# Tile 24's normalizer steps made one tile later in a one-core attention decode kernel

## The chip, the cores and the metric

The kernel runs on one core of a Trainium2 chip. The metric is the device time of one execution in microseconds (us), as the median of several runs. Beside it stands one execution taken by the hardware profiler, with every instruction of the five engines: TensorE (PE; PEld is its weight load), VectorE (DVE), ScalarE (ACT), GpSimd (POOL) and SyncE (SP, which here only issues DMAs). Times inside the profile count from the start of its span.

## The reference

One transformer layer for one new token in each of four batch rows: a condition vector gives shifts, scales and gates; attention over a cache of 4096 keys and values for 32 heads of 128; then a small gated MLP. Nearly all work and nearly all bytes are in the attention:

```python
q = (h @ wq).reshape(B, 1, 32, 128).transpose(0, 2, 1, 3)
scores = einsum('bhqd,bhkd->bhqk', q, k_cache) * 128 ** -0.5
p = softmax(scores, axis=-1)
o = einsum('bhqk,bhkd->bhqd', p, v_cache)
x = x + ga * (o.reshape(B, 1, 4096) @ wo)
x = x + gb * mlp(layernorm(x) * (1 + cb) + sb)
```

Everything is bf16. The two caches are 4 x 32 x 4096 x 128 values each, 268 MB together; the whole kernel reads 282.73 MB from HBM.

## The kernel before

The attention is cut into `NT` = 32 tiles. A tile is 4.19 MB of keys and as much of values, laid out as 128 partitions x 128 keys x 128 (`NJ` = 128 keys in each partition). The first `N0` = 24 tiles come in pairs: tiles 2k and 2k+1 together are 8 heads of one batch row, their scores are made one tile after the other and their softmax and value product once for the pair (after the odd tile). Tiles 24 to 31 are single: 4 heads each, with a softmax and a value product of their own. Tile 24 is the first of these.

The order of the work on every engine is the order in which the program's lines issue it (a manual schedule): one loop over the tiles from line 701. Each engine takes its own list in order, and an instruction that waits holds up those behind it on that engine alone. In iteration i the steps that matter here are:

- `mult(i, 0)`, `mult(i, 1)` (L393, VectorE): keys times query, half a tile (64 keys) each, 128 x 8192 elements.
- `reduce_d` (L401, TensorE): sums products over part of the head dimension into a PSUM tile `red`; `sum8` (L424, VectorE) finishes the sum into the score tile `S`; `sum_rest` (L413, VectorE) sums the last 48 keys of the tile without TensorE.
- `scores(i - 1)` (L437 to L454, VectorE): row maximum and what the exponential needs; it then calls `exps`.
- `exps` (L467, ScalarE): the exponentials, written as bf16 into the weight tile `pbd`, with their row sums into `rs`. Pairs use the whole of `pbd`; single tiles use a quarter of it each, and need the rest to be zero.
- `pv` (L519, TensorE): the value product. `PV_START`, `PV_MID` and `PV_END` say in which iteration it stands.
- `norm_r` (single tiles: L487, VectorE, `rsb` = `maskd` times `rs`; pairs: L481, POOL), `norm_a` (L497, TensorE, sums `rsb` over partitions into `z`) and `norm_b` (L504, VectorE, the reciprocal `rz`). `o_scale` (L566 for single tiles) multiplies the value product by `rz`. These three steps are what the change moves.

Before the change `norm_r(i - 1)` and `norm_a(i - 1)` stand in iteration i, and `norm_b(i - 2)` near its start. Iteration 25 is special, because the layout of `pbd` changes there from pairs to single tiles: the value product of the last pair (`PV_MID`, tile 23) must have read `pbd`, then POOL sets it to zero (L732), and only then the exponentials of tile 24 are issued; `scores(24)` has left them out:

```python
if i in PV_MID:
    pv(PV_MID[i])
if i == N0 + 1:
    load_v(N0)
    load_v(N0 + 1)
    nc.gpsimd.memset(pbd8, 0.0)
    nc.vector.memset(opss[0], 0.0)
    exps(N0)
```

All bulk loads are issued by SP on one queue, in the order of the `load_...` calls; each waits on SP until its buffer is free. Keys go into buffers `bufA` and `bufB` in turn (8.39 MB each), values into `bufC`; the values of tiles 30 and 31 go into `bufB` behind the keys of tiles 30 and 31, and the weights of the end (`wo`, `win`, `wout`, `wg`) into `bufA`. The last loads in the queue are, in order: the values of tile 30 (4.19 MB), those of tile 31 in five pieces (32, 32, 32, 16 and 16 keys: 1.05 MB three times, 0.52 MB twice), `win` in two (0.92 MB each, L602), `wout` (0.92 MB, L603) and `wg` in two (0.39 and 0.13 MB, L605).

After the loop comes the tail: the last scores, value products and the projection with `wo` (`o_last` L555, `o_proj` L613), the second layer norm, the MLP's first product with `win` (L884), its second with `wout` (L909), the gate `gb` from `wg` (L917), some ten small VectorE steps to L954, and the output's DMA (L955).

Of the kernel before, what the change touches and what calls it, by code (L numbers as in the profile page):

```python
# [54 lines left out]
def kernel(  # L55
# [32 lines left out]
    N0 = 2 * B * GP  # L88
# [25 lines left out]
    def ps_sm(shape, dtype=F32):  # L114
        return psum.tile(shape, dtype, name="sm", bufs=3)
# [42 lines left out]
    def load_v(i):  # L158
        if i < N0:
            load(bufC, kv_view(A_v_cache, i), (NP,))  # L160
        else:
            load(vts[i], kv_view(A_v_cache, i), TAIL if i == L else (NJ,))
# [220 lines left out]
    def pair(i):  # L383
        return i < N0

    def ends(i):
        return i >= N0 or i % 2 == 1

    def mult(i, kc):
        kt = kts[i][:, kc * KC:(kc + 1) * KC, :]  # L390
        g, b = divmod(i // 2 if pair(i) else i - N0, B)
        q = (qbp if pair(i) else qbo)[:, g, b, :]
        nc.vector.tensor_tensor(out=kt, in0=kt, in1=bc(q, KC), op=ALU.mult)  # L393

    def reduce_d(i, kc):
        ns = on_pe(i, kc)
        rd = 512 // ns
        kt = kts[i][:, kc * KC:kc * KC + ns, :]
        red = ps_red().rearrange("p (n r) -> p n r", r=rd)
        for m in range(DH // rd):  # L400
            nc.tensor.matmul(  # L401
                red, lhsT=ident_bf, rhs=kt[:, :, m * rd:(m + 1) * rd],
                start=(m == 0), stop=(m == DH // rd - 1),
            )
        st[i, "red", kc] = red
# [23 lines left out]
    def scores(i):  # L429
        sum8(i, 1)  # L430
        S = st.pop((i, "S"))
        if not ends(i):
            return
        if pair(i):
            S = st["both"]
        mrow = wk.tile([P, 1], F32, name="mrow")
        nc.vector.tensor_reduce(out=mrow, in_=S, axis=AX.X, op=ALU.max)  # L437
        mb = wk.tile([P, R], F32, name="mb", bufs=1)
        if pair(i):
            nc.vector.scalar_tensor_tensor(  # L440
                out=mb, in0=mrow.to_broadcast([P, R]), scalar=-att_scale,
                in1=fars.rearrange("p h u -> p (h u)"), op0=ALU.mult, op1=ALU.add,
            )
        else:
            nc.vector.tensor_scalar(
                out=mb, in0=mrow.to_broadcast([P, R]), scalar1=-att_scale, scalar2=None, op0=ALU.mult
            )
        mt = wk.tile([P, R], F32, name="mt", bufs=1)
        nc.vector.transpose(mt, mb)
        nM = wk.tile([P, 1], F32, name="nM")  # L450
        nc.vector.tensor_reduce(out=nM, in_=mt, axis=AX.X, op=ALU.min)  # L451
        if pair(i):
            nb = wk.tile([P, 2], F32, name="nb")
            nc.vector.tensor_scalar(out=nb, in0=far, scalar1=nM, scalar2=None, op0=ALU.add)  # L454
            nM = nb
        st[i, "in"] = S, nM
        if i != N0:
            exps(i)
# [14 lines left out]
    def norm_r(i):  # L473
        if not ends(i):
            return
        rs = st.pop((i, "rs"))
        if pair(i):
            g, b = divmod(i // 2, B)
            if b == 0:
                st["P", g, "rsb"] = wk.tile([P, B, HQ, 2], F32, name="rsb8")  # L480
            nc.gpsimd.tensor_tensor(  # L481
                out=st["P", g, "rsb"][:, b], in0=maskd[:, :, None].to_broadcast([P, HQ, 2]),
                in1=rs[:, None, :].to_broadcast([P, HQ, 2]), op=ALU.mult,
            )
            return
        st[i, "rsb"] = wk.tile([P, HQ], F32, name="rsb")
        nc.vector.tensor_scalar(out=st[i, "rsb"], in0=maskd, scalar1=rs, scalar2=None, op0=ALU.mult)  # L487

    def norm_a(i):
        if not pair(i):  # L490
            rsb = st.pop((i, "rsb"))
        elif i % (2 * B) == 2 * B - 1:
            rsb = st.pop(("P", i // 2 // B, "rsb")).rearrange("p b q h -> p (b q h)")
        else:
            return
        z = ps_sm(list(rsb.shape))
        nc.tensor.matmul(z, lhsT=inv_d, rhs=rsb, start=True, stop=True)  # L497
        st[i, "z"] = z

    def norm_b(i):  # L500
        if (i, "z") in st:
            z = st.pop((i, "z"))
            rz = wk.tile(list(z.shape), F32, name=f"rz{z.shape[1]}", bufs=2 if pair(i) else 4)
            nc.vector.reciprocal(out=rz, in_=z)  # L504
            st[i, "rz"] = rz
# [4 lines left out]
    def pv(i):  # L510
        n = (NP if pair(i) else NJ) // G
        pv_some(i, 0, n, n)
# [11 lines left out]
    def o_pick(i):  # L524
        ops = ops_of(i)
        sel = sels[HP if pair(i) else HQ]
        osb = wk.tile([P, DH], F32, name="osb", bufs=2)
        nc.vector.tensor_scalar(  # L528
            out=osb, in0=ops[:, 0, :], scalar1=sel[:, 0:1], scalar2=None, op0=ALU.mult
        )  # L530
        for g in range(1, G):
            nc.vector.scalar_tensor_tensor(  # L532
                out=osb, in0=ops[:, g, :], scalar=sel[:, g:g + 1], in1=osb,
                op0=ALU.mult, op1=ALU.add,
            )
        st[i, "osb"] = osb
# [109 lines left out]
    def dealt(k):  # L646
        pp = st.pop(("pp", k))
        n = pp.shape[1]
        ow = own if n == HP else own[:, 0:n * B, 0:n]
        nc.vector.tensor_tensor(  # L650
            out=ow, in0=pp.rearrange("p r b h -> p (r b) h"),
            in1=bc(mask8 if n == HP else mask4, n * B), op=ALU.mult,
        )
        od = late.tile([P, n, B], BF16, name=f"od{k}")
        with nc.allow_low_precision("all but one term of each sum are zero"):
            nc.vector.tensor_reduce(
                out=od.rearrange("p r b -> p (r b)"), in_=ow, axis=AX.X, op=ALU.add
            )
        st["od", k] = od
# [31 lines left out]
    def o_add(wp, b0, b1):  # L691
        a = acc[:, :, b0:b1]
        nc.vector.tensor_tensor(out=a, in0=a, in1=wp, op=ALU.add)
# [3 lines left out]
    def add_up():  # L697
        while adds:
            o_add(*adds.pop(0))

    for i in range(NT):
        mult(i, 0)
        if i >= 1:
            scores(i - 1)
        if i >= 2:
            norm_b(i - 2)
        todo = PICKS.get(i, (i - 3,) if i % 2 == 0 and 4 <= i <= N0 + 2 else ())
        t = PV_START.get(i, i - 2 if i % 2 and 3 <= i < N0 else None)
        if t is not None:
            pv(t)  # L710
        if i % 2 and i < N0:
            load_v(i)
        if i == L:
            dealt(1)
            dealt(2)
        reduce_d(i, 0)
        for t in todo:
            o_pick(t)
            o_cols(t)
        if i == 0:  # L720
            late_mod_b()
        if i == N0 + 2:
            nc.vector.memset(opss[1], 0.0)
        if i == L:
            project()
            deal(GP)
# [8 lines that stand above are left out]
        if i == L - 1:  # L735
            deal(0)
        mult(i, 1)
        if i >= 1:
            norm_r(i - 1)
        for t in todo:  # L740
            o_scale(t)
        sum8(i, 0)
        if i == L - 1:
            dealt(0)
        if i == L:
            rows_out()
            dealt(GP)
            o_pick(L - 3)
        reduce_d(i, 1)
        sum_rest(i)  # L750
        if i >= 1:
            norm_a(i - 1)
        if i == L - 1:
            deal(1)
            deal(2)
        if i == L:
            o_cols(L - 3)
            turn()
        if i in PV_END:
            if i == N0 + 3:  # L760
                load_v(N0 + 2)
            pv(PV_END[i])
        if i == L:
            o_scale(L - 3)
        if i % 2 and i + 3 < N0:
            load_k(i + 3)
        elif i == N0 - 3 or i == N0 - 1 or i == N0 + 1:
            load_k(i + 3)
            load_k(i + 4)
        elif i == N0 + 3:  # L770
            load_v(N0 + 3)
            load_k(L - 1)
            load_k(L)
        elif i == L - 2:
            load_wo()
            late_consts()
            load_v(L - 3)
            load_v(L - 2)
        elif i == L - 1:
            load_v(L - 1)  # L780
        elif i == L:
            load_v(L)
            load_end()
# [202 lines left out]
```

## Time and profile before

| | |
|---|---|
| median of 3 runs | 668.81 us (668.15 to 669.12) |
| the profiled execution | 668.59 us, its span 666.8 us |
| VectorE busy | 577.0 us (87% of the span), 437 instructions |
| TensorE busy | 315.9 us (47%), weight loads 137.1 us (21%) |
| ScalarE, GpSimd busy | 154.9 us (23%), 18.5 us (3%) |
| the bulk-load queue | 282.73 MB, its packets 98.4% of 16 engines' span |
| mean granted TensorE clock | 0.75 of full speed |

The profiled execution lies 1.79 us above its span; that remainder is outside what the profile sees. Busy shares are means over the whole span, so they do not say which engine a stage waits for; that is read from the idle time ahead of an instruction, which the trace prints in square brackets with what ended it ("[6.63 <-ACT pbd L467]": idle for 6.63 us until ScalarE's L467 was done).

### The profile page before, as it was taken

How to read it: one execution, taken by the hardware profiler on the slowest of the kernel's cores; microseconds unless marked ns; L12 is line 12 of the kernel's file. 1: busy time of each engine (PE TensorE's matmuls, PEld its weight loads, DVE VectorE, ACT ScalarE, POOL GpSimd, SP SyncE). 2: the span in 40 equal slices, each digit the busy share in tenths (PEclk: the TensorE clock that was granted, in tenths of full speed). 3: DMA queues.
4: the chain of work that ended last, by engine and by line, in shares of the span. 5: the costliest groups of instructions: out<-in, count | busy, mean ns of one | idle time of the engine just before them, and what ended most of it. 6: DMA issues, size and time to landing. Idle time of an engine off the chain costs nothing.

```text
span 666.8 us, 5276 instructions
## 1 busy us (share of the span) xinstructions
PE 315.9 (47%) x2136; PEld 137.1 (21%) x2136; DVE 577.0 (87%) x437; ACT 154.9 (23%) x287; POOL 18.5 (3%) x55
## 2 busy tenths in 40 slices
PE   1565363645253464524245452524536144544996
PEld 0222121212021121211112120211212012221445
DVE  3249999999898998989799897989997799999934
ACT  1210605032050604114060410506060111111112
POOL 3000000000000000000000000000000000004000
PEclk9988787867568786756778675777876688776986
DMA  8999999999999999999999999999999999999994
GB/s 362 452 441 413 440 437 437 433 441 441 436 436 429 418 436 440 433 429 434 436 440 433 436 426 429 441 440 410 440 440 420 436 426 429 439 419 433 437 413 167
DMA packets 10222, 283.09 MB, mean 425 GB/s; under 512 B 972, under 2 KB 2900, under 8 KB 4052
## 3 DMA queue, kind: packets, MB, share of 16 engines
q1 hardware_dynamic: 10176, 282.73, 98.4%
q8 instruction: 17, 0.28, 0.1%
q14 instruction: 9, 0.07, 0.0%
q10 hardware_dynamic: 20, 0.01, 0.0%
HBM read 282.73 MB, written 0.00 MB: 424 GB/s over the span
## 4 chain that ended last, share of the span: by engine, by line
DMA 46%; DVE 35%; PE 15%; ACT 3%; issue 1%; POOL 0%; SPq 0%; DVEq 0%; ACTq 0%
DMA bC<-in_A_v_cache_dram 29%; DMA bB<-in_A_k_cache_dram 12%; DVE S L413 12%; DVE bB L393 10%; PE ops L519 8%; DVE bA L393 6%; PE red L401 3%; DMA bC<-in_w_mod_dram 3%; DVE S L424 2%; ACT pbd L467 2%; DVE osb L532 2%; DMA bC<-in_B_b_sp_dram 1%; PE sm L668 1%; PE qps L326 1%; PE sm L318 1%
## 5 line engine op out<-in xcount | busy, mean ns | idle before, releaser
L467 ACT ACTIVATE pbd<-S,nb 32x256 bf16<-32x256 f32 x96 | 123.5, 1520 | 338.4 <-DVE nb L454 311.1
L401 PE MATMUL red<-bB,ident_bf 128*128 128x512 bf16 x344 | 97.9, 443 | 123.8 <-DVE bB L393 123.8
L401 PE MATMUL red<-bA,ident_bf 128*128 128x512 bf16 x332 | 96.7, 451 | 124.4 <-DVE bA L393 124.4
L401 PEld LDWEIGHTS <-ident_bf 128*128 128x128 bf16 x676 | 74.3, 111 | 364.7 <-issue 232.4
L393 DVE TENSOR_TENSOR bA<-bA,qbp 128x8192 bf16<-128x8192 bf16 x24 | 105.9, 4413 | 19.7 <-DMA bA<-in_A_k_cache_dram 19.7
L393 DVE TENSOR_TENSOR bB<-bB,qbp 128x8192 bf16<-128x8192 bf16 x24 | 106.0, 4418 | 11.2 <-DMA bB<-in_A_k_cache_dram 11.2
L519 PE MATMUL ops<-bC,pbd 128*32 128x512 bf16 (+1 forms) x960 | 79.7, 502 | 54.8 <-DMA bC<-in_A_v_cache_dram 49.7
L413 DVE TENSOR_REDUCE S<-bA 128x48 f32<-128x6144 bf16 x15 | 98.1, 6543 | 0.0
L413 DVE TENSOR_REDUCE S<-bB 128x48 f32<-128x6144 bf16 x14 | 91.6, 6544 | 0.0
L519 PEld LDWEIGHTS <-pbd 128*32 128x32 bf16 (+1 forms) x1008 | 34.1, 119 | 99.8 <-issue 50.0
L467 ACT ACTIVATE pbd<-S,nM 32x128 bf16<-32x128 f32 x32 | 18.5, 578 | 123.6 <-DVE nM L451 80.3
L467 ACT ACTIVATION_READ_ACCUMULATOR pbd<-S,nb 32x1 f32 x96 | 46.9, 489 | 0.0
L424 DVE TENSOR_REDUCE S<-red 128x64 f32<-128x512 f32 x64 | 43.7, 684 | 2.2 <-PE red L401 2.2
L393 DVE TENSOR_TENSOR bA<-bA,qbo 128x8192 bf16<-128x8192 bf16 x8 | 35.3, 4412 | 0.0
L393 DVE TENSOR_TENSOR bB<-bB,qbo 128x8192 bf16<-128x8192 bf16 x8 | 35.3, 4412 | 0.0
L481 POOL TENSOR_TENSOR rsb<-maskd,rs 128x8 f32<-128x8 f32 x12 | 2.4, 200 | 490.7 <-ACT pbd L467 490.7
L532 DVE SCALAR_TENSOR_TENSOR osb<-ops,m,osb 128x128 f32<-128x128 f32 x36 | 12.6, 351 | 1.3
L497 PE MATMUL sm<-rsb,inv_d 128*128 128x4 f32 (+1 forms) x22 | 4.5, 280 | 15.8 <-POOL rsb L481 12.0
L532 DVE SCALAR_TENSOR_TENSOR osb<-ops,selg,osb 128x128 f32<-128x128 f32 x24 | 8.4, 351 | 0.8
L528 DVE TENSOR_SCALAR osb<-ops,selg 128x128 f32<-128x128 f32 x8 | 2.7, 340 | 6.8 <-PE ops L519 6.8
L497 PEld LDWEIGHTS sm<-rsb,inv_d 128*128 128x128 f32 x22 | 4.7, 236 | 18.8 <-POOL rsb L481 13.5
L467 ACT ACTIVATION_READ_ACCUMULATOR pbd<-S,nM 32x1 f32 x32 | 8.1, 252 | 0.0
(164 smaller groups left out, 157.9 us busy)
## 6 DMA issues: line engine op xcount, KB each, us to landing
bA<-in_A_k_cache_dram SPq DMA_DIRECT2D x6, 4096.0 KB, 37.3
bC<-in_A_v_cache_dram SPq DMA_DIRECT2D x6, 4096.0 KB, 28.0
bB<-in_A_k_cache_dram SPq DMA_DIRECT2D x3, 4096.0 KB, 36.9
bC<-in_A_wq_dram SPq DMA_DIRECT2D x1, 4096.0 KB, 12.5
bB<-in_A_k_cache_dram SPq DMA_DIRECT2D x2, 2048.0 KB, 37.0
bB<-in_A_v_cache_dram SPq DMA_DIRECT2D x1, 4096.0 KB, 19.1
bA<-in_A_wo_dram SPq DMA_DIRECT2D x3, 1024.0 KB, 31.2
bB<-in_A_v_cache_dram SPq DMA_DIRECT2D x3, 1024.0 KB, 17.9
```

The lines of the kernel that those rows point to most:

```text
L318: nc.tensor.matmul(qr[R * q:R * (q + 1)], lhsT=hT[:, k, :], rhs=wq_v[:, k, gs, q, :], start=(k == 0), stop=(k == DJ - 1), tile_position=(0 ...
L326: nc.tensor.matmul(qp[:, 0:npair], lhsT=eb2[k][:, b].rearrange("p k q r -> p (k q r)"), rhs=qrow[:, h, k:2 * npair:2], start=(k == 0), sto ...
L393: nc.vector.tensor_tensor(out=kt, in0=kt, in1=bc(q, KC), op=ALU.mult)
L401: nc.tensor.matmul(red, lhsT=ident_bf, rhs=kt[:, :, m * rd:(m + 1) * rd], start=(m == 0), stop=(m == DH // rd - 1),)
L413: nc.vector.tensor_reduce(out=st[i, "S"][:, n0:NJ], in_=kts[i][:, n0:NJ, :], axis=AX.X, op=ALU.add)
L424: nc.vector.tensor_reduce(out=st[i, "S"][:, kc * KC:kc * KC + on_pe(i, kc)], in_=st.pop((i, "red", kc)), axis=AX.X, op=ALU.add,)
L467: nc.scalar.activation(out=pbd8[r, :, 2 * q + h] if pair(i) else pbds[r, i % 4, :, q], in_=S[r, :], func=AF.Exp, bias=nM[r, h:h + 1], scal ...
L497: nc.tensor.matmul(z, lhsT=inv_d, rhs=rsb, start=True, stop=True)
L519: nc.tensor.matmul(ops_of(i)[g:g + rows], lhsT=pb[:, n, :], rhs=vt[:, n, :], start=(m < 4), stop=(m >= end - 4), tile_position=(0, g),)
L528: nc.vector.tensor_scalar(out=osb, in0=ops[:, 0, :], scalar1=sel[:, 0:1], scalar2=None, op0=ALU.mult)
L532: nc.vector.scalar_tensor_tensor(out=osb, in0=ops[:, g, :], scalar=sel[:, g:g + 1], in1=osb, op0=ALU.mult, op1=ALU.add,)
L668: nc.tensor.matmul(wp, lhsT=od[:, r, :], rhs=wo_sb[:, k * HP + r, :], start=(k == 0 and r == 0), stop=(k == GP - 1 and r == HP - 1),)
```

## The change

For tile 24 alone, `norm_r`, `norm_a` and `norm_b` are issued one iteration later, with those of tile 25 and ahead of them. `normed_in(i)` lists the tiles whose product and sum are issued in iteration i: none in iteration 25, tiles 24 and 25 in iteration 26, and i - 1 in every other. The reciprocals follow one iteration behind: tile 24's is made in iteration 27 instead of 26. Nothing is added or removed. Lines below the new function move by five.

```diff
+    def normed_in(i):
+        if i <= 0 or i == N0 + 1:
+            return ()
+        return (i - 2, i - 1) if i == N0 + 2 else (i - 1,)
+
     for i in range(NT):
         mult(i, 0)
         if i >= 1:
             scores(i - 1)
-        if i >= 2:
-            norm_b(i - 2)
+        for k in normed_in(i - 1):
+            norm_b(k)
...
         mult(i, 1)
-        if i >= 1:
-            norm_r(i - 1)
+        for k in normed_in(i):
+            norm_r(k)
         for t in todo:
             o_scale(t)
         sum8(i, 0)
...
         reduce_d(i, 1)
         sum_rest(i)
-        if i >= 1:
-            norm_a(i - 1)
+        for k in normed_in(i):
+            norm_a(k)
```

## The prediction

> **What bounds the kernel now.** I read first the stages around the change, as busy time, granted TensorE clock, DMA share and bytes per stretch (columns: stretch; its length; busy us and instruction count of PE, PEld, DVE, ACT and POOL; clock; DMA share; GB/s):
>
> ```profile
> 447.20:513.40 66.20, 29.83 (x168) 12.17 (x172) 65.39 (x44) 20.62 (x32) 0.40 (x2) 0.70 1.00 430
> 513.40:520.10 6.70, 3.31 (x48) 1.26 (x40) 0.07 (x2) 2.30 (x8) 1.80 (x1) 1.00 1.04 450
> 520.10:600.00 79.90, 35.58 (x223) 15.22 (x224) 78.81 (x64) 9.27 (x32) 0.00 (x0) 0.74 1.00 429
> 600.00:641.00 41.00, 30.52 (x186) 14.89 (x189) 34.96 (x52) 5.98 (x21) 7.05 (x8) 0.82 1.01 429
> 641.00:654.00 13.00, 10.15 (x135) 4.83 (x128) 5.65 (x22) 1.01 (x4) 0.00 (x0) 0.76 1.01 418
> 654.00:658.80 4.80, 3.80 (x64) 3.53 (x65) 1.88 (x11) 0.82 (x4) 1.04 (x5) 0.50 0.70 250
> ```
>
> Two things are full. VectorE is busy 65.39 of 66.20 us before 513.4 and 78.81 of 79.90 after 520.1, and in the 6.70 us between it does nothing. The 16 DMA engines are full throughout (share 1.00 to 1.04 up to 654), in the very gap too. Two chains thus run side by side at almost one pace: the list of VectorE, and the stream of bytes.
>
> The timeline of that gap gives its cause (start, us, engine, line; in brackets the idle time before and what ended it):
>
> ```profile
> 509.03 4.41 DVE L393 TENSOR_TENSOR bA<-bA,qbo 128x8192 bf16<-128x8192 bf16 x1
> ...
> 512.11 3.64 PE L519 MATMUL ops<-bC,pbd 128*32 128x512 bf16 x64
> ...
> 515.82 1.80 POOL L732 MEMSET pbd<- 128x2048 bf16 x1 [15.71 <-PE ops L519]
> ...
> 519.45 0.57 ACT L467 ACTIVATE pbd<-S,nM 32x128 bf16<-32x128 f32 x1
> ...
> 520.06 0.23 DVE L487 TENSOR_SCALAR rsb<-maskd,rs 128x4 f32<-128x4 f32 x1 [6.63 <-ACT pbd L467]
> 520.20 0.68 DVE L424 TENSOR_REDUCE S<-red 128x64 f32<-128x512 f32 x1
> ...
> 520.80 6.54 DVE L413 TENSOR_REDUCE S<-bA 128x48 f32<-128x6144 bf16 x1
> ```
>
> Tile 24's product (L487) is VectorE's next instruction after `mult(25, 1)`, and needs row sums that come only when tile 23's value product has read `pbd` (to 515.8), POOL has cleared it (517.6) and ScalarE has made four exponentials (520.0). Behind it stand L424 and L413, whose inputs were ready: the sum on TensorE ended at 512.17.
>
> Last the end of the stream: the issues of the last loads with their time from issue to landing, and what SP's queue waited for.
>
> ```profile
> bA<-in_B_w_in_dram SPq DMA_DIRECT2D x2, 896.0 KB, 14.3
> ...
> bA<-in_B_w_out_dram SPq DMA_DIRECT2D x1, 896.0 KB, 16.5
> bA<-in_w_mod_dram SPq DMA_DIRECT2D x1, 384.0 KB, 15.1
> ...
> bA<-in_w_mod_dram SPq DMA_DIRECT2D x1, 128.0 KB, 12.9
> ```
>
> SP issued `wout` at 640.99 and `wg` at 643.44 and 645.94 (SP's timeline), so these land at 657.5, 658.5 and 658.8. The same SP rows were held, by the table of SP's waits, until values of tiles 30 and 31 had landed: tile 30 at 640.99, the first two pieces of tile 31 at 643.4 and 645.9.
>
> **The change, step by step.** *Removed:* the stall. VectorE goes from `mult(25, 1)` (ends 513.44) straight to L424 and L413: -6.63 us on its list. L424 carries a wait on ScalarE in the changed program's list, because its score buffer was tile 23's two tiles back; those exponentials ended at 499.8. That this kind of wait is for two tiles back and not for tile 24 shows in the same step one tile earlier: L424 at 495.19 ran without idling while ScalarE was in the middle of tile 23's exponentials (489.4 to 499.8). So 0.
>
> *Moved:* one L487 (0.13 us of list, from 539.66 to 539.79), one pair of PE passes (L497, 0.28 us) and one reciprocal (L504, 0.09 us) go one tile later; each is still done once, so VectorE's sum does not change. In their new place L487 stands behind `mult(26, 1)`, which ends about 533; both tiles' exponentials are done by then (tile 24's at 520.0, tile 25's some 2.4 us after their start near 526.8). The reciprocals stand 11 us behind their PE passes, and `o_scale` of tile 24 wants the result another tile later (578.1 before). No DMA moves and SP's list is unchanged. Cost 0; were the cover gone, the price would be these rows, 0.5 us.
>
> *What is late next.* With VectorE 6.63 us earlier, do the keys still come in time? Counting back from tile 30's values at 641.0, one tile's 4.19 MB at 429 GB/s being 9.78 us: keys 26 land at 513.9 (wanted at 527.26 - 6.63 = 520.6), keys 27 at 523.7 (540.7), keys 28 at 553.0 (558.2), 29 at 562.8 (578.7), 30 at 592.1 (596.2), 31 at 601.9 (611.8). Values 24 and 26 land at 533.4 and 572.5 for value products that would start at 534.2 and 572.9; TensorE's next work for VectorE is 7 us behind the end of each, so a short wait there costs nothing. So VectorE keeps its 6.63 us to the end of tile 31.
>
> There the stream takes over. It is full in every stretch before 654, always with one or two loads waiting in the queue, so earlier issues do not make a byte land sooner, and the last loads keep their landing times. What each allows against its user in the old trace:
>
> - values of tile 30: 641.0, used by L519 at 646.42: 5.4 us
> - second piece of tile 31: 645.94; its matmuls are the last 8 of a group of 48 (646.35 to 650.80), so they begin about 650.1: 4.1 us
> - third piece: not shown; 1.05 MB behind the second at 418 GB/s, 648.4, used at 652.17: 3.7 us, of which 0.6 us is forgiven, since TensorE then idles 0.7 us before L226
> - `wout`: 657.5, used by L909 at 661.56: 4.06 us
> - `wg`: 658.8; its last four matmuls would run about 662.7 and are wanted by VectorE's L950 at 663.59: 3.9 to 4.4 us
>
> So the least is 4.06 us, at `wout`, and the end moves by -4.06 instead of -6.63; the rest turns into waits for DMA in the tail. Small waits that meet (pieces 2 and 3, `wout`) may cost 0.1 us more: I take -4.0. Bounds for this step: -6.63 (no landing in the way), and nothing (below). In the profiled execution's own time 668.59 - 4.0 = 664.6; the median shown is 0.22 higher, so **664.8 us**.
>
> The Trainium skill (DMA: Bandwidth & Descriptors, Specifications) gives the 16 engines a ceiling of 435 GB/s. Stretches here average 418 to 450, so the trace roughly agrees. By that figure the 7.47 MB behind tile 30's values would take 17.2 us instead of the 17.8 seen (641.0 to 658.8), and the sum would be -4.6 at most: the page speaks against the whole 6.63.
>
> **Rivals.** *The stall pays in full*, 668.81 - 6.63 = 662.2. It needs the last loads to land 2.6 us sooner. For it: the last 3 us of the stream run at 0.70 of the engines' share, and some of that might close up. Against it: share 1.00 for 200 us; a fuller queue has nothing to fill. 12 in 100.
>
> *No difference* (within 0.2%, that is 1.34 us, about what a measurement of this kernel can tell from no change), 668.2. Now the end hangs on landings, so a stream 0.4% slower (2.7 of 659 us) eats the 4.0 down to 1.3; or the stall stays whole because L424's wait is for tile 24 after all (668.8, 3 in 100, against the row at 495.19). For it: stretches differ by several per cent. Against: the stream is given the same loads in the same order. 12 in 100.
>
> *Slower*, by one mechanism: TensorE's granted clock between 622.9 and 651. The row of that clock stands at 1.00 from 622 to 638 and at 0.50 after 654. Groups of one kind cost more at the lower clock: a value product of 32 matmuls 1.90 us against 3.34, 16 sums 3.61 against 4.90 to 6.35. In the tail TensorE would now stand idle for landings. If that stage ran at the lower clock throughout: one value product +1.4, two sums of 16 +2.6 to +5.5, the projection's 24 matmuls +2.0 to +4.1, together +6.0 to +11.0. It decides once it exceeds the 6.63 pulled forward, and gives 668.2 to 673.2, say 670.5. Against it: the waits for landings come after 640, behind this stage, and everything ahead moves together. 6 in 100. The Trainium skill (TensorE: Matmul & The Clock Gate, Part 1) says the array runs at half clock until activity releases it, which would be the cause; the trace's 0.50 in idle stretches agrees.
>
> **How the numbers follow.** Forecast 70 in 100 (its own range 663.6 to 666.4: -5.2 to -2.4), full gain 12, no difference 12, slower 6. Faster by over 0.2%: 82; within: 12; slower: 6. The range, 662.2 to 667.2, takes in the full gain and, on the other side, a stream 0.36% slower than before (2.4 us of 659) on top of the forecast.
>
> **What would show it.** Right: no idle time before L424 of tile 25; VectorE's `mult(31, 1)` at about 619.6 instead of 626.2; new waits for DMA on TensorE at the values of tiles 30 and 31 and at `wout`; the last landing still near 658.8 with some 4 us behind it instead of 8. Wrong: a landing of `wg` near 656 (full gain), or the last landing moved later, or VectorE idle before keys 28 or 30.

## The result, and the profile after

The changed kernel takes 664.74 us (median of 6 runs, 664.6 to 666.45) against 668.37 us before (6 runs, 668.15 to 669.12): the ratio is 0.9948, 95% interval 0.9935 to 0.9961. The profiled execution takes 664.6 us with a span of 662.8 us; before it was 668.59 and 666.8. So the span is 4.0 us shorter and the median 3.6 us (by the interval 2.6 to 4.3), where the stall that was taken away was 6.63 us long.

VectorE's timeline in iterations 25 and 26 (start, us, engine, line) no longer shows a gap:

```profile
508.85 4.41 DVE L393 TENSOR_TENSOR bA<-bA,qbo 128x8192 bf16<-128x8192 bf16 x1
513.18 0.68 DVE L424 TENSOR_REDUCE S<-red 128x64 f32<-128x512 f32 x1
513.77 6.54 DVE L413 TENSOR_REDUCE S<-bA 128x48 f32<-128x6144 bf16 x1
...
532.57 0.35 DVE L487 TENSOR_SCALAR rsb<-maskd,rs 128x4 f32<-128x4 f32 x2
```

L424 and L413 follow `mult(25, 1)` at once, without a bracket, and both tiles' products stand together at 532.57, again without a wait. The second half of the last tile's keys (`mult(31, 1)`) is reached at 619.26 instead of 626.20, 6.9 us sooner; 0.2 us of that were there ahead of the change (508.85 against 509.03).

The stages of the changed kernel, in the same stretches as before (length; busy us of PE, PEld, DVE, ACT, POOL; clock; DMA share; GB/s):

```profile
513.40:520.10 6.70, 3.25 (x48) 1.31 (x41) 6.70 (x2) 2.31 (x8) 1.80 (x1) 1.00 1.03 445
520.10:600.00 79.90, 35.82 (x223) 15.37 (x223) 78.81 (x64) 9.27 (x32) 3.88 (x4) 0.76 1.00 429
600.00:641.00 41.00, 34.53 (x218) 16.46 (x218) 30.17 (x59) 6.97 (x24) 3.16 (x5) 0.83 1.01 429
641.00:654.00 13.00, 9.39 (x156) 6.20 (x156) 5.18 (x24) 0.50 (x2) 1.05 (x5) 0.76 1.02 419
654.00:658.80 4.80, 4.07 (x105) 3.67 (x106) 2.03 (x11) 3.77 (x8) 0.00 (x0) 0.50 0.69 242
```

VectorE now works through the first of them (6.70 of 6.70 us). The DMA columns are the old ones within 4%: 429, 429 and 419 GB/s where there were 429, 429 and 418. The stream of bytes landed when it had before: SP issued tile 30's values 6.9 us sooner (at 615.07 instead of 621.92), and they landed at 641.0 both times. What moved is the work around it, and TensorE's timeline in the tail shows where the two meet:

```profile
641.04 3.60 PE L519 MATMUL ops<-bB,pbd 128*16 128x512 bf16 x40 [1.49 <-DMA bB<-in_A_v_cache_dram]
645.90 0.61 PE L519 MATMUL ops<-bB,pbd 128*16 128x512 bf16 x8 [1.25 <-DMA bB<-in_A_v_cache_dram]
...
648.35 0.96 PE L555 MATMUL qps<-pbd,bB 128*128 128x4 bf16 x32 [0.61 <-DMA bB<-in_A_v_cache_dram]
...
650.79 0.59 PE L555 MATMUL qps<-pbd,bB 128*128 128x4 bf16 x16 [0.46 <-DMA bB<-in_A_v_cache_dram]
...
657.48 0.91 PE L914 MATMUL qps<-bC,bA 128*128 128x8 bf16 x28
```

The same places in the kernel before:

```profile
646.35 4.45 PE L519 MATMUL ops<-bB,pbd 128*16 128x512 bf16 x48
...
652.17 0.94 PE L555 MATMUL qps<-pbd,bB 128*128 128x4 bf16 x32
...
655.13 0.57 PE L555 MATMUL qps<-pbd,bB 128*128 128x4 bf16 x16
...
661.56 0.89 PE L909 MATMUL qps<-bC,bA 128*128 128x8 bf16 x28
```

Four groups of products that waited for no DMA before now wait for values of tiles 30 and 31, and the MLP's second product (L914, L909 before) starts at 657.48. Its weights were issued at 641.02 and took 16.4 us to land: 657.4. The chain that ended last says the same (start, us, what): from the issue of tile 30's values to L914 it is only transfers. A transfer's time here runs from its issue to its landing, with the wait in the queue in it.

```profile
615.07 25.93 DMA bB<-in_A_v_cache_dram
641.00 0.02 issue
641.02 16.42 DMA bA<-in_B_w_out_dram
657.44 0.04 issue
657.48 0.93 PE qps L914 x28
```

In the tail of the kernel before, this chain ran through TensorE and VectorE instead: L519 at 646.42, o_pick's L528 at 649.37, and so on without a transfer.

### The profile page after: what moved, and what is told of

Its sections match the earlier page's. It is cut to its first block, busy times and chain, and to the rows that moved or that the text cites. A ratio compares the mean times of both kernels' runs of the same rounds, so it can differ in the third digit from the quotient of the medians.

```text
span 662.8 us, 5277 instructions
## 1 busy us (share of the span) xinstructions
PE 319.0 (48%) x2136; PEld 137.6 (21%) x2136; DVE 576.8 (87%) x437; ACT 154.8 (23%) x287; POOL 18.5 (3%) x55
## 4 chain that ended last, share of the span: by engine, by line
DMA 52%; DVE 34%; PE 10%; ACT 2%; issue 1%; SPq 0%; DVEq 0%
DMA bC<-in_A_v_cache_dram 29%; DMA bB<-in_A_k_cache_dram 13%; DVE S L413 12%; DVE bB L393 10%; DVE bA L393 6%; PE ops L519 6%; DMA bB<-in_A_v_cache_dram 4%; DMA bC<-in_w_mod_dram 3%; DMA bA<-in_B_w_out_dram 2%; DVE S L424 2%; PE red L401 2%; ACT pbd L467 2%; DMA bC<-in_B_b_sp_dram 1%; DVE osb L532 1%; PE qps L326 1%
## 5 line engine op out<-in xcount | busy, mean ns | idle before, releaser
L519 PE MATMUL ops<-bC,pbd 128*32 128x512 bf16 (+1 forms) x960 | 81.0, 509 | 54.7 <-DMA bC<-in_A_v_cache_dram 49.6
L413 DVE TENSOR_REDUCE S<-bA 128x48 f32<-128x6144 bf16 x15 | 98.1, 6541 | 0.0
L413 DVE TENSOR_REDUCE S<-bB 128x48 f32<-128x6144 bf16 x14 | 91.6, 6542 | 0.0
L519 PEld LDWEIGHTS <-pbd 128*32 128x32 bf16 (+1 forms) x1008 | 34.5, 121 | 103.5 <-issue 54.5
L424 DVE TENSOR_REDUCE S<-red 128x64 f32<-128x512 f32 x64 | 43.6, 682 | 2.0 <-PE red L401 2.0
L528 DVE TENSOR_SCALAR osb<-ops,selg 128x128 f32<-128x128 f32 x8 | 2.7, 340 | 8.6 <-PE ops L519 8.6
L497 PE MATMUL sm<-rsb,inv_d 128*128 128x4 f32 (+1 forms) x22 | 4.3, 281 | 12.1 <-POOL rsb L481 12.0
L437 DVE TENSOR_REDUCE mrow<-S 128x1 f32<-128x256 f32 (+1 forms) x20 | 7.3, 366 | 0.7
```

What stands on the lines that cost most here:

```text
L413: nc.vector.tensor_reduce(out=st[i, "S"][:, n0:NJ], in_=kts[i][:, n0:NJ, :], axis=AX.X, op=ALU.add)
L424: nc.vector.tensor_reduce(out=st[i, "S"][:, kc * KC:kc * KC + on_pe(i, kc)], in_=st.pop((i, "red", kc)), axis=AX.X, op=ALU.add,)
L519: nc.tensor.matmul(ops_of(i)[g:g + rows], lhsT=pb[:, n, :], rhs=vt[:, n, :], start=(m < 4), stop=(m >= end - 4), tile_position=(0, g),)
L528: nc.vector.tensor_scalar(out=osb, in0=ops[:, 0, :], scalar1=sel[:, 0:1], scalar2=None, op0=ALU.mult)
```

## The experiments

The theory: two chains run side by side. VectorE's list set the end before, and the last loads landed some 4 us before they were wanted; the change takes 6.6 to 6.9 us from the list, the stream becomes the later one, and keeps 2.6 us or more. The rivals: (a) the stream set the end already; (b) VectorE's list sets it in both kernels and the stall was only worth 4 us; (c) something else in the tail, TensorE's clock above all, keeps the missing part; (d) the later places of TensorE's sum and of the reciprocal have a share in it. Two levers tell these apart, each pulled in both kernels: bytes in the stream, and work on VectorE. The runs are called E1 to E10, each at its result. The kernel before was run along with each group of them: 668.59 us with E1 to E4, 668.83 with E5 to E8 and 668.79 with E9 and E10. Its single runs reach from 667.6 to 671.5 us. The changed kernel was not run again, so a difference from its 664.74 us compares runs of different groups, and half a microsecond there says little.

**Fewer bytes.** Two of the three 1.05 MB groups of `wo` are not loaded, and the projection reads the first group three times.

```diff
         for n in (HP,) * GP + (HQ,):
+            if h0 in (HP, 2 * HP):
+                h0 += n
+                continue
             nc.sync.dma_start(
...
-                    wp, lhsT=od[:, r, :], rhs=wo_sb[:, k * HP + r, :],
+                    wp, lhsT=od[:, r, :], rhs=wo_sb[:, r, :],
```

> The kernel before without the loads of two of the three 1.05 MB groups of wo (the projection reads the first group three times, so the output is not the reference's). The stream ends 2.1 MB, some 4.9 us, sooner. Theory (the stream was hidden behind VectorE's list in the kernel before, by about 4 us): no change, 668.4 us (667.9 to 668.8). Rival (the end of the kernel before hung on the stream already): 663.5 to 665.

Measured (E1): 668.73 us, ratio 1.0003 (0.9993 to 1.0012). In the trace tile 30's values land at 636.2 instead of 641.0, `wout` at 654.0 instead of 657.5 and the last of `wg` at 655.2 instead of 658.8. So the end of the stream came 3.6 us sooner, not 4.9; `wout` was issued at 640.77, almost as late as before (640.99). Landings 3.5 to 4.8 us sooner are worth nothing in the kernel before; rival (a) falls.

> The changed kernel with the same two loads left out. Theory (the stream took over and keeps 2.6 us of the 6.63 us): with 4.9 us fewer in the stream the whole stall is paid, 668.4 - 6.63 to - 6.9 = 661.5 to 661.8 us, no DMA wait ahead of the products with the values of tiles 30 and 31, and none ahead of the MLP's second product. Rival (TensorE at a lower clock or another wait in the tail keeps the 2.6 us): 664.7 us as the changed kernel.

Measured (E2): 662.14 us, ratio 0.9900 (0.9886 to 0.9914), 6.4 us under the kernel before in its group and 0.3 above what was expected; the span is 660.4 us, 6.4 us shorter as well. TensorE's timeline of this run, at the places that waited in the changed kernel:

```profile
639.20 4.32 PE L519 MATMUL ops<-bB,pbd 128*16 128x512 bf16 x48
...
645.51 0.98 PE L555 MATMUL qps<-pbd,bB 128*128 128x4 bf16 x32
...
654.97 0.89 PE L917 MATMUL qps<-bC,bA 128*128 128x8 bf16 x28
```

All 48 products stand in one group again, nothing waits for a DMA, and the MLP's second product comes at 654.97. The part of the stall that was missing is back as soon as the stream is shorter, which (b) does not give. In this trace the value product of tile 29 also took 2.37 us, 1.05 less than in the changed kernel's trace, so a part could be TensorE's. But in E8 below that product took 1.90 us, and TensorE only waited the longer for tile 30's values (1.69 us, until 641.03); the MLP's second product started at 657.60. A faster TensorE gains nothing while the stream is as long as it was, and (c) falls too.

**More bytes.** The first part of `win` (0.92 MB) is loaded once more, ahead of tile 30's values.

```diff
         elif i == L - 1:
+            extra = B_w_in.rearrange("(p j) n -> p j n", p=P)
+            nc.sync.dma_start(out=win_sb[:, KIN[0]], in_=extra[:, KIN[0]])
             load_v(L - 1)
```

> The kernel before with the first 0.92 MB of win loaded twice, the extra time ahead of the values of tile 30: 2.1 us more in the stream (the result is the same). Theory (the stream has about 4 us to spare in the kernel before): nothing to 0.2 us, 668.4 to 668.6 us. Rival (bytes cost the same in both kernels): 670.5 us.

Measured (E5): 668.47 us, ratio 0.9988 (0.9975 to 1.0001): free, as expected, although in the trace tile 30's values landed at 643.3 and `wout` at 659.8, both 2.3 us later.

> The changed kernel with the same extra load. Theory (the stream sets the end): the whole 2.1 us, 666.9 us, with the last weights landing at about 660.9 instead of 658.8. Rival (VectorE's list or TensorE's clock sets it): 664.7 us.

Measured (E6): 666.87 us, ratio 0.9961 (0.9947 to 0.9975), 2.1 us more than the changed kernel's 664.74 and 1.8 more than E8's 665.09 in the same group (666.65 to 667.36 against 664.68 to 665.57). The first wait in the tail has grown by 2.4 us and the second product starts 2.2 us later:

```profile
643.02 4.07 PE L519 MATMUL ops<-bB,pbd 128*16 128x512 bf16 x40 [3.90 <-DMA bB<-in_A_v_cache_dram]
...
659.64 0.91 PE L916 MATMUL qps<-bC,bA 128*128 128x8 bf16 x28 [0.18 <-DMA bA<-in_B_w_out_dram]
```

**More work on VectorE.** The sum over the last 16, 32 or 48 keys of tile 28 is made a second time, with the same result (here 16).

```diff
         sum_rest(i)
+        if i == N0 + 4:
+            nc.vector.tensor_reduce(
+                out=st[i, "S"][:, NJ - 16:NJ], in_=kts[i][:, NJ - 16:NJ, :], axis=AX.X, op=ALU.add
+            )
```

> The kernel before with the sum over the last 16 keys of tile 28 made twice on VectorE: 16/48 of a 6.54 us row, 2.2 us more in its list (the result is the same). Theory (VectorE's list sets the end of the kernel before): the whole 2.2 us, 670.6 us. Rival (the stream sets it in both kernels): 668.4 to 669.

Measured (E3): 671.11 us, ratio 1.0036 (1.0023 to 1.0049): +2.5 us for a row of 2.29 us. By the medians it is paid in full. In the single trace two other things partly offset each other: the stall ahead of L487 is 7.39 us, 0.8 more than in the kernel before's, and the value product of tile 29 takes 1.90 us, 1.4 less.

> The changed kernel with the same 2.2 us more on VectorE. Theory (its list now runs 2.6 us ahead of what the stream lets the tail use): nothing to 0.3 us, 664.7 to 665.0 us, with shorter DMA waits in the tail. Rival (VectorE's list still sets the end, and the stall was worth only 4 us): 666.9 us.

Measured (E4): 664.44 us, ratio 0.9938 (0.9925 to 0.9952): nothing. The wait for tile 30's values has shrunk from 1.49 to 0.61 us, and its product starts where it did, at 640.97 instead of 641.04:

```profile
640.97 3.95 PE L519 MATMUL ops<-bB,pbd 128*16 128x512 bf16 x40 [0.61 <-DMA bB<-in_A_v_cache_dram]
```

The traced run is the slowest of the five (665.83 us), but it issues the output's DMA at 660.41, where the changed kernel does at 660.55; what it has more lies behind that. That 2.3 us more on VectorE cost the product only 0.9 us of its waiting time has a reason that the next run made plain.

> The changed kernel with the sum over the last 32 keys of tile 28 made twice, 4.4 us more in VectorE's list (the result is the same). Theory: the first 2.6 to 2.9 us are free, the rest shows: 664.7 + 1.5 to 1.8 = 666.2 to 666.5 us. Rival (VectorE's list sets the end throughout): 669.1 us; (only the stream sets it): 664.7 us.

Measured (E7): 665.45 us, ratio 0.9942 (0.9919 to 0.9964): 0.7 us over the changed kernel, where the theory had said 1.5 to 1.8. The expectation missed. By the ratios to the kernel before in each group (0.9948 for the changed kernel, 0.9942 here) the added work cost nothing that can be told from noise, and in the trace it cost nothing at all: the MLP's second product starts at 657.42. VectorE's list was as late as computed (`mult(31, 1)` at 623.54, 4.3 us behind the changed kernel), but the value product of tile 29 ahead of tile 30's took 1.90 us; in the changed kernel it took 3.42. First the row of this run, then that of the changed kernel:

```profile
638.00 1.90 PE L519 MATMUL ops<-bC,pbd 128*16 128x512 bf16 x32
```

```profile
633.71 3.42 PE L519 MATMUL ops<-bC,pbd 128*16 128x512 bf16 x32
```

The same 32 matmuls ran at another granted clock (1.00 over 626 to 642 here, 0.76 over 631 to 638 there), and TensorE made up 1.5 us of what VectorE lost. So by an estimate from these rows the list has 4.1 to 4.4 us to spare when the clock falls that way, not 2.6 to 2.9. Two more runs were to tell this from a theory that VectorE's time is just cheap after the change.

> The changed kernel with the whole 48-key sum of tile 28 made twice, 6.6 us more in VectorE's list, which puts that list back to where the kernel before has it (the result is the same). Theory (VectorE's list sets the end as soon as it is less than some 4 us ahead of the old one; the 4.4 us run came out 1.5 us short of that because the value product of tile 29 ran at the full granted clock, 1.90 us instead of 3.42): 668.6 us where that product takes 3.4 us, 667.1 us where it takes 1.9 us. Rival (more VectorE work is nearly free in the changed kernel, 0.7 us for 4.4): at most 666 us.

Measured (E9): 668.29 us, ratio 0.9986 (0.9974 to 0.9998). With VectorE's list put back to its old place (`mult(31, 1)` at 626.08, 626.20 in the kernel before), the gain is gone but for 0.1%. Its 11 runs reach from 667.14 to 669.04 us, four of them below 667.4 and six above 668.2, near the two values expected for the two clocks. That this is the clock is not shown: only one run (668.48) has a trace, and there the product took 2.53 us, between the two.

> The kernel before with the sum over the last 32 keys of tile 28 made twice, 4.4 us more on VectorE (the result is the same). Theory: 668.6 + 4.4 = 673.0 us, or 671.6 us where the value product of tile 29 takes 1.9 us. Rival (as above, nearly free): 669.3 us.

Measured (E10): 673.38 us, ratio 1.0066 (1.0050 to 1.0082): +4.6 us for a row of 4.42 us, all of it. In the traced run the value product of tile 29 took 1.90 us, which should have saved 1.4 us; but its VectorE list lost 6.5 us up to `mult(31, 1)` where 4.4 were added, 0.7 of them in a longer stall ahead of L487 (7.36 us) and 0.8 in two waits of L424 for sums on TensorE, so the two offset each other. The six runs lie at 672.6 to 672.8 and at 674.0 to 674.4, three each, and the traced one (674.15) is of the slower three with the product at the higher clock; so that product alone does not part them.

**One line alone.** The product of tile 24 stays in iteration 25 and only steps behind the two sums; TensorE's sum and the reciprocal stay where they were.

```diff
-        if i >= 1:
+        if i >= 1 and i != N0 + 1:
             norm_r(i - 1)
...
         sum_rest(i)
+        if i == N0 + 1:
+            norm_r(N0)
```

> The kernel before with one line moved: tile 24's product stays in iteration 25, but stands after the 48-key sum instead of before the two sums; its TensorE sum and reciprocal stay in their iterations. By then (520.2 us) the exponentials it waits for (to 520.0) are done. Theory (the whole effect is that VectorE's list was held by one instruction at its head): the same time as the changed kernel, 664.7 us. Rival (the later place of TensorE's sum and of the reciprocal is part of it): between 664.7 and 668.4 us.

Measured (E8): 665.09 us, ratio 0.9931 (0.9909 to 0.9953), span 662.9 us in the trace against 662.8: the changed kernel again. Rival (d) falls; the tile of delay is not needed, only a place behind work that is ready.

## Why the prediction was right

- *The stall goes, 6.63 us of VectorE's list:* right; at `mult(31, 1)` it is 6.9 us, 0.2 of them the run's own. The wait that L424 takes on cost nothing, as the step one tile earlier had shown.
- *The moved steps cost nothing:* right; L487, L497 and L504 of tile 24 stand in rows without a wait. E8 shows that the place of the last two does not matter.
- *Keys and values still come in time:* right. VectorE waits for no key after tile 24, and of the value products of tiles 24 to 29 only one waited: the values of tile 26, put at 572.5 for a start at 572.9, were waited for 0.28 us (start at 572.84), at no cost.
- *The stream takes over at the end, -4.06 us at `wout`:* right in the place and the size. Landings are the old ones within 0.1 us (tile 30's values 641.0, `wout` 657.4), and the second product moved from 661.56 to 657.48, 4.08 us; the last VectorE step moved by 4.00. E2 and E6 show the stream as the cause, from both sides.
- *The ceiling of the Trainium skill (DMA: Bandwidth & Descriptors, Specifications):* it put the gain at 4.6 us at most with the loads as they are. 4.0 us and the 419 GB/s from 641 to 654 agree with it, and E2 passed it only by having fewer bytes. Over the 6.70 us from 513.4 the traces show 450 and 445 GB/s, a little above the page's figure; there the measurement decides.
- *The rival with the full gain* would have needed a faster end of the stream; the last 4.8 us moved 242 GB/s, 250 before. *No difference* and *slower* did not come: the stage from 615 to 631, which is the old 622 to 638, has its granted clock of 1.00 again.
- That the forecast of 664.8 lies within 0.1 us of the median is in part luck. The sum goes from the 668.81 of three runs, the median before is 668.37 with six, and the medians are 3.63 us apart instead of 4.0.
- What the prediction had too simple is not in its sum: it took stall and slack from one trace. The stall is 6.63 to 7.39 us long in the five traces that have it, and in the tail of the trace that was used one group of matmuls happened to run slowly. With that group at the higher clock the tail's own chain is 1.5 us shorter (E7), and a kernel before that ran so would by this estimate gain about 2.6 us from the change, not 4.06. The time of the changed kernel hardly depends on it, since the stream sets the end: E8 had that group at 1.90 us, and took 665.09.

## What to carry to other kernels

An engine's stall is worth its length only until the next chain becomes the later one: put the landing time of each late transfer beside its first user, and the smallest difference is the most that a saving ahead of it can give while the transfers stay where they are. To learn which chain sets the end, add a known amount to each and see which one is paid: here 2.1 us of bytes were free before and cost 2.1 after, and 2.3 us of VectorE cost 2.5 before and nothing after. And an instruction that waits for a long chain belongs behind the work on its engine that is ready; a few places in the list do, it need not be a whole iteration.

## What was not expected of the hardware

One group of 32 identical matmuls (the value product of tile 29) took 1.90 us in six of the twelve traces (E3, E4, E6, E7, E8, E10) and 2.37 to 3.43 us in the other six, although the same few small matmuls stand ahead of it in all of them. The granted clock was 1.00 in E7 (626 to 642), 0.76 in the changed kernel (631 to 638) and 0.50 in the kernel before (640.5 to 643.2). The 16 sums on TensorE ahead of tile 23's value product vary in the same way, and the stall that the change removes varies with them: 5.46 us of sums at a clock of 0.63 (506 to 512) and a stall of 6.63 in the kernel before, 6.23 at 0.50 and 7.39 in E3. The Trainium skill (TensorE: Matmul & The Clock Gate, Part 1) says that the window over which the array's activity is judged runs free, so one kernel meets it at different points; the traces agree with that, but no run here set the phase on purpose. For this kernel it means some 1.5 us, 0.2%, that come and go where TensorE's work lies on the path to the end, as in the kernel before. Whether it parts the times of E9 and E10 stays open, as only one run of each has a trace.
